# A fused attention and gated feed-forward kernel: a new order of the loads, the beginning and the first eight tiles

## The chip, the cores and the metric

The kernel runs on one core of a Trainium2 chip. The metric is the device time of one execution in microseconds (us). The core has five engines that work at the same time, each through its own list of instructions in order: TensorE (PE, products), VectorE (DVE), ScalarE (ACT), GpSimd (POOL) and SyncE (SP), which issues the loads and the transposes by DMA. Engines wait for each other by semaphores.

## The reference

```python
kv_pool = kv.reshape(B, H//4, 4, W//4, 4, C).mean(axis=(2, 4))
k = v = kv_pool.reshape(B, -1, C) @ w_sr            # 768 keys per batch
a = softmax(q @ k.T / sqrt(C));  x = a @ v          # 4 batches x 12288 rows, C = 128
x_prev = x shifted by one row (0 at a batch's start)
xk = mu_k*x + (1-mu_k)*x_prev;   xr = mu_r*x + (1-mu_r)*x_prev
out = sigmoid(xr @ w_r) * (relu(xk @ w_k)**2 @ w_v) # w_k 128x1024, w_v 1024x128
```

All of it is in float32; the kernel splits operands into a high and a low half and adds three products where one would lose digits.

## The kernel before

The 4 x 12288 rows are worked through in 96 tiles of 512 rows (the last one as two halves). Each tile is cut into small steps, each a named closure: `qf` loads the rows, `qh` and `ql` split them, `S0` to `S3` (with `SA0`, a first part) are the score products for four groups of 128 rows, `nm` is the row maximum on DVE, `ex` the exponential on ACT, `rc` the reciprocal sum, `f1` and `f2` split the softmax into two halves (tile `pp`), `tt` transposes `pp` by DMA into `pT`, `AV0` to `AV5` multiply it with the values (tile `px`), `xk` and `xr` mix neighbouring rows, `ha`, `hb`, `va`, `vb` and `z` are the feed-forward products, `o` and `so` the output.

No loop sets the order. Every step is put into one heap with a number, and `plan.give()` takes them out by that number; the engines' lists follow. The numbers stand in tables: `ONCE` for what is done once, `EARLY` for the first eight tiles (one dictionary each), `WHEN` plus 19.3 per tile for the tiles after, `LATE` for the last. The numbers are only a sequence, not times.

What is done once is of four kinds. Weights: `L_wk0`, `L_wk1`, `L_wv0`, `L_wv1` (512 KB each) and `L_wr0` (128 KB) are loaded as 64-bit words and put together on ACT and DVE (`wb`, `wl`, `wf`, `wu`, `ws`, `wt`, `we`, `wq`, `wp`); `wa` takes magnitudes (tile `wabs`) and `wc` sums their columns on PE into the PSUM tile `cs`; `wx` reads the largest sums from `cs` on DVE (tile `peak`). Keys of batch 0, the first 512 columns: `L_a0` to `L_a7` (512 KB each), each multiplied on PE as it lands (`pa0` to `pa7`, two products of two passes of 512 columns each), all into one sum. The other 256 columns: `L_b0` to `L_b2` (512 KB) and `L_b3`, `L_b4` (256 KB) are added up by DVE (`ab0` to `ab4`, tile `acc`) and multiplied afterwards (`pk1` for 192 columns, `pk2` for 64). From the key products ACT and DVE make `ks`, `ksh`, `kbl`; the exponent chain `ex` (five instructions on single columns, up to the reciprocal `ivs`) follows the maxima `am`. The key loads share six buffers: the seventh load waits until the first buffer has been read.

The fourth kind does no work of the reference: `id0`, `id1` and so on are products of the identity with itself, written into a part of `cs` that nobody reads.

```python
for j in range(IDLE):
    @once(f"id{j}")
    def _():
        for n in range(2):
            pe.matmul(column_sums(1), lhsT=ident, rhs=ident, start=True, stop=True)
...
dve.tensor_reduce(out=one("peak", n=3), in_=column_sums(), axis=AX.X, op=ALU.max)
```

`column_sums(1)` is the second half of `cs` and `column_sums()` a part of the first; both are one tile, so a product of `idN` that stands after `wx` waits until DVE has read. In float32 each such product is two passes of PE, so one `idN` is four.

Of the kernel before, what the change touches and what calls it, by code (L numbers as in the profile page):

```python
# [73 lines left out]
def tile_kernel(ctx, tc, qT, kv0a, kv0b, kvw, head, w_k, w_v, w_r, outT):  # L74
# [91 lines left out]
    def once(name):  # L166
        def put(fn):
            plan.add(ONCE[name], name, fn, ("once", 0))
        return put
# [31 lines left out]

    for j in range(IDLE):
        @once(f"id{j}")
# [871 lines left out]
    for i, (b, t0, T, at0) in enumerate(seq):  # L1075
# [26 lines left out]
IDLE = 24  # L1102
# [84 lines left out]
        "xek": 60.09518, "xk": 62.09518, "xkh": 68.09518, "xer": 72.09518, "xr": 82.09518,  # L1187
# [9 lines left out]
    },  # L1197
    {
# [7 lines left out]
        "AV5": 110.09518, "xcr": 114.09518, "xek": 129.09518, "xer": 130.09518, "xk": 137.09518,  # L1206
        "xr": 138.09518, "xkh": 149.09518, "xkl": 163.09518, "ha2": 188.49961, "xrh": 188.55182,
# [8 lines left out]
    },  # L1216
    {
# [270 lines left out]
```

## Time and profile before

| | |
|---|---|
| median of 3 runs | 1856.12 us (1855.11 to 1856.93) |
| span of the profiled execution, first to last instruction | 1854.3 us |
| PE busy | 1839.3 us, 9079 products |
| DVE, ACT, POOL busy | 1730.9, 1743.0, 1133.2 us |
| DMA | 252.52 MB, mean 136 GB/s |
| granted TensorE clock, mean | 1.000 |

The page gives the profiled execution's span, not its time by the runs' clock; a run's time also holds what lies around the span, and the median is 1.8 us above this span. Busy times are sums of one engine's instructions; where two engines are nearly full at once, a wait of one stage can still decide. Products are pipelined, so a row's duration is longer than the distance to the next one.

### The profile page before, as it was taken

The page shows a single profiled execution, that of the slowest core. Times are in us where ns is not written, and L with a number is a line of the kernel's source. Part 1 is how long each engine was busy: PE and PEld are TensorE (multiplying, and loading weights), DVE is VectorE, ACT ScalarE, POOL GpSimd, SP SyncE. Part 2 cuts the span into 40 slices and gives each one's busy share as a digit, 9 for nine tenths or more (in the row PEclk, how much of TensorE's full clock was granted, in tenths as well). Part 3 has the DMA queues.
Part 4 walks back from the last instruction along what each step waited for, and adds up shares of the span by engine and source line. Part 5 has one row for each costly group of instructions (what it writes and reads, how often), then busy time and mean ns, then how long its engine had stood idle before and what let it go on. Part 6 is the DMA issues. An engine that isn't in the chain of part 4 may idle for free.

```text
span 1854.3 us, 27743 instructions
## 1 busy us (share of the span) xinstructions
PE 1839.3 (99%) x9079; PEld 912.5 (49%) x9185; DVE 1730.9 (93%) x2811; ACT 1743.0 (94%) x2628; POOL 1133.2 (61%) x875
## 2 busy tenths in 40 slices
PE   9999999999999999999999999999999999999999
PEld 6444454444444444444444444444444444444445
DVE  8999999999999999999999999999998999899898
ACT  6999999999999999999999999999999999999997
POOL 1655565666666566666666666656666666666666
PEclk9999999999999999999999999999999999999999
DMA  7677575656667676656666676747565656555462
GB/s 248 142 154 160 130 166 125 129 128 131 135 138 168 142 159 148 134 118 128 137 127 164 142 170 141 161 103 142 123 136 120 128 128 125 120 109 114 91 126 57
DMA packets 654336, 252.52 MB, mean 136 GB/s; under 512 B 612080, under 2 KB 613104, under 8 KB 654192
## 3 DMA queue, kind: packets, MB, share of 16 engines
q1 hardware_dynamic: 654192, 250.75, 63.1%
q8 instruction: 72, 1.18, 0.3%
q14 instruction: 72, 0.59, 0.1%
HBM read 73.34 MB, written 25.17 MB: 53 GB/s over the span
## 4 chain that ended last, share of the span: by engine, by line
PE 89%; ACT 2%; issue 1%; DVE 0%; DVEq 0%; ACTq 0%
PE ph L39 25%; PE pv L39 24%; PE S L39 19%; PE px L39 18%; PE pz L39 3%; ACT rr L39 0%; ACT kh L39 0%; ACT pp L39 0%; PE pk L39 0%; ACT pe L39 0%; ACT kk L39 0%; ACT S L39 0%; ACT xer L39 0%; DVE pp L39 0%; DVE kk L39 0%
## 5 line engine op out<-in xcount | busy, mean ns | idle before, releaser
L39 POOL TENSOR_TENSOR kl<-kk,kh 128x1024 bf16<-128x1024 f32 (+1 forms) x291 | 617.9, 2124 | 129.4 <-ACT kh L39 112.6
L39 ACT ACTIVATE rr<-ph 128x1024 f32<-128x1024 f32 (+1 forms) x388 | 395.8, 1021 | 80.0 <-PE ph L39 76.8
L39 PE MATMUL px<-pT,vT 128*128 128x512 f16 (+1 forms) x1746 | 391.8, 377 | 2.1 <-DMA pT<-pp 2.1
L39 POOL TENSOR_TENSOR xrl<-xr,xrh 128x512 f16<-128x512 f32 (+1 forms) x97 | 144.9, 1494 | 275.1 <-DVE xrh L39 275.1
L39 ACT ACTIVATE kh<-rr 128x1024 f16<-128x1024 f32 (+1 forms) x291 | 306.5, 1055 | 0.7 <-PE pv L39 0.2
L39 PE MATMUL S<-kf,qh 128*128 128x256 f16 x1264 | 304.3, 326 | 0.0
L39 PE MATMUL ph<-xkh,wkl 128*128 128x512 f16 (+1 forms) x776 | 292.0, 377 | 0.4 <-DVE kk L39 0.2
L39 PE MATMUL pv<-kh,wvl 128*128 128x512 f16 (+1 forms) x776 | 291.9, 377 | 0.1
L39 PE MATMUL ph<-xkh,wkh 128*128 128x512 f16 (+1 forms) x776 | 291.9, 377 | 0.0
L39 PE MATMUL pv<-kh,wvh 128*128 128x512 f16 (+1 forms) x776 | 291.8, 377 | 0.0
L39 DVE SCALAR_TENSOR_TENSOR pp<-pe,rc,pp 128x768 f16<-128x768 f32 x289 | 286.9, 1011 | 0.5 <-ACT pp L39 0.5
L39 PEld LDWEIGHTS <-vT 128*128 128x128 f16 x1746 | 170.4, 98 | 205.9 <-issue 3.1
L39 ACT ACTIVATE pp<-pe,rc 128x768 f16<-128x768 f32 x289 | 263.8, 952 | 1.6 <-DVE rc L39 1.6
L39 DVE TENSOR_SCALAR_CACHE_REDUCE pe<-S,gs 128x768 f32<-128x768 f32 x238 | 238.0, 1015 | 25.5 <-PE S L39 25.4
L39 POOL TENSOR_TENSOR ql<-qf,qh 128x512 f16<-128x512 f32 (+2 forms) x97 | 141.9, 1463 | 195.1 <-ACT qh L39 195.1
L39 ACT ACTIVATE pe<-pe,nm 128x768 f32<-128x768 f32 x265 | 248.0, 936 | 0.3 <-DVE pe L39 0.3
L39 PEld LDWEIGHTS <-wkh 128*128 128x128 f16 x1552 | 151.8, 98 | 178.4 <-issue 0.7
L39 DVE TENSOR_TENSOR kk<-ph,rr 128x1024 f32<-128x1024 f32 (+1 forms) x194 | 233.9, 1206 | 3.9 <-ACT rr L39 3.2
L39 PE MATMUL ph<-xkl,wkh 128*128 128x512 f16 (+1 forms) x776 | 228.6, 377 | 0.0
L39 PE MATMUL S<-kf,ql 128*128 128x256 f16 x632 | 205.9, 326 | 4.1
L39 POOL TENSOR_TENSOR xkl<-xk,xkh 128x512 f16<-128x512 f32 (+1 forms) x97 | 145.1, 1496 | 103.0 <-DVE xkh L39 103.0
L39 PE MATMUL pv<-kl,wvb 128*128 128x512 bf16 (+1 forms) x681 | 193.0, 377 | 0.5
(152 smaller groups left out, 2937.5 us busy)
## 6 DMA issues: line engine op xcount, KB each, us to landing
qf<-qT SPq DMA_DIRECT2D x95, 256.0 KB, 3.6
outT<-o SPq DMA_DIRECT2D x95, 256.0 KB, 3.4
qm<-qT SPq DMA_DIRECT2D x78, 256.0 KB, 3.6
kvt<-kvw SPq DMA_DIRECT2D x36, 512.0 KB, 4.9
pT<-pp SPq DMA_TRANSPOSE x383, 4.0
kva<-kv0a SPq DMA_DIRECT2D x8, 512.0 KB, 9.4
kvb<-kv0b SPq DMA_DIRECT2D x3, 512.0 KB, 6.0
land<-moe_w_k SPq DMA_DIRECT2D x2, 512.0 KB, 6.2
```

The costliest lines, as they stand in the source:

```text
L39: return self.tc.keep_in_program_order(op(*args, **kwargs))
```

## The change

The instructions are the same; `IDLE` goes from 24 to 25, and the tables `ONCE` and `EARLY` get new numbers. `WHEN`, `LATE` and all code stay.

```diff
-IDLE = 24
+IDLE = 25
...
-    "id16": -145.90482, "id17": -144.90482, "id18": -143.90482, "id19": -142.90482,
...
-    "L_wk1": -137.90482, "L_b3": -136.90482, "mix": -135.90482, "L_wr0": -134.90482,
...
+    "L_wk1": -149.03887, "wb_wk1": -148.07774, "id0": -147.11661, "id1": -146.15548,
...
+    "id13": -41.39230, "pk1": -40.43117, "ks1": -39.47004, "am1": -38.50891, "ex": -37.54778,
+    "kb0": -36.58665, "wc_wv0": -35.62552, "wx": -34.66439, "id14": -33.70326, "id15": -32.74213,
```

The loads stood in the order wk1, b3, wr0, b4, a4, wv1, wk0, a6, a3, a7, wv0, a5, a0, a1, b2, a2, b1, b0; they now stand in the order wk1, wr0, wv1, b4, a6, b3, a3, wk0, a7, a5, a4, wv0, a2, a1, b2, b1, a0, b0. The eight key blocks are multiplied in the order a4, a6, a3, a7, a5, a0, a1, a2 before and a6, a3, a7, a4, a5, a2, a1, a0 now. The steps `idN` stood as 8 at the start, 3, 4 and 3 up to the first scores, then 3, 2 and 1 (24); they now stand as 9, 2, 1, 2 and 3, then 3, 2, 1 and 2 (25).

DVE's list near its beginning, before: the sums `ab3` and `ab4` (`acc<-kvb 128x32`) stand first, around a few instructions of the weights.

```order
L39 MEMSET mtop 128x1
L39 TENSOR_REDUCE acc<-kvb 128x32 [waits DMAHW2_49]
L39 TENSOR_SCALAR sign<-land 128x512 [waits DMAHW1_49]
L39 TENSOR_SCALAR mag<-mag 128x128 [waits Activation_49]
L39 TENSOR_SCALAR mag<-mag 128x128 [waits DVE_49]
L39 TENSOR_SCALAR mag<-mag 128x512 [waits Activation_49]
L39 TENSOR_SCALAR mag<-mag 128x512 [waits DVE_49]
L39 TENSOR_REDUCE acc<-kvb 128x32 [waits DMAHW4_49]
```

The same place now, with the end of what stands in front of them; PE's product on these sums (`pk2`) and the load `L_a4`, into the buffer of `L_b4`, wait for the second.

```order
L39 MEMSET mtop 128x1
L39 TENSOR_SCALAR mag<-mag 128x512 [waits Activation_49]
L39 TENSOR_SCALAR ei<-top 128x512
L39 TENSOR_SCALAR mag<-mag 128x512 [waits DVE_49]
L39 SCALAR_TENSOR_TENSOR top<-mag,sign 128x512 [waits DVE_49]
L39 TENSOR_TENSOR lf<-lf,ei 128x128
L39 TENSOR_SCALAR ei<-top 128x512 [waits DVE_49]
L39 TENSOR_REDUCE acc<-kvb 128x32 [waits DMAHW6_49]
L39 TENSOR_REDUCE acc<-kvb 128x32 [waits DMAHW4_49]
```

So 25 instructions of the weights and of `mix`, eight of them on 512 columns with one input and two with two inputs, moved ahead of the two sums.

PE's list in front of the first score product, before: the identity products (`cs<-ident`, six are three steps) wait for nothing.

```order
L39 MATMUL cs<-ones,wabs 128x1
L39 MATMUL cs<-ident 128x128 x6
L39 LDWEIGHTS ql [waits Pool_49]
L39 MATMUL S<-kbl,ql 128x512 [waits Activation_49]
L39 MATMUL S<-ksh,qh 128x512
L39 LDWEIGHTS qh
L39 MATMUL S<-kbl,qh 128x512 [waits DVE_49]
```

And now; all four groups of column sums stand ahead of it.

```order
L39 MATMUL cs<-ones,wabs 128x1
L39 MATMUL cs<-ident 128x128 [waits DVE_49]
L39 MATMUL cs<-ident 128x128 x5
L39 LDWEIGHTS ql [waits Pool_49]
L39 MATMUL S<-kbl,ql 128x512 [waits Activation_49]
L39 MATMUL S<-ksh,qh 128x512
L39 LDWEIGHTS qh
L39 MATMUL S<-kbl,qh 128x512
```

The first identity product now waits for DVE, and the score products stand behind it.

What it waits for stands on DVE here: `peak<-cs`, before, behind the first three row maxima (`nm<-S`).

```order
L39 RECIPROCAL ivs<-exs 128x1 [waits DVE_49]
L39 SCALAR_TENSOR_TENSOR kbl<-pk,ksh 128x192 [waits Activation_49]
L39 TENSOR_REDUCE nm<-S 128x1 [waits PE_49] x3
L39 TENSOR_REDUCE peak<-cs 128x3
L39 TENSOR_SCALAR rc<-sm 128x2 [waits Activation_49]
```

And now, behind the reciprocal of the exponent chain.

```order
L39 SCALAR_TENSOR_TENSOR kbl<-pk,ksh 128x512 [waits Activation_49]
L39 TENSOR_REDUCE tip<-ks 128x1 [waits Activation_49] x2
L39 TENSOR_REDUCE ex<-tip 128x1 [waits DVE_49]
L39 TENSOR_SCALAR ex<-ex 128x1 [waits DVE_49]
L39 TENSOR_SCALAR exi<-ex 128x1 [waits DVE_49]
L39 TENSOR_SCALAR exs<-exi 128x1 [waits DVE_49]
L39 RECIPROCAL ivs<-exs 128x1 [waits DVE_49]
L39 TENSOR_REDUCE peak<-cs 128x3 [waits PE_49]
L39 SCALAR_TENSOR_TENSOR kbl<-pk,ksh 128x192 [waits Activation_49]
L39 TENSOR_REDUCE nm<-S 128x1 [waits PE_49] x3
```

The reading of the column sums moved ahead of the three row maxima, and with it the place for which PE waits.

## Rows read from the trace of the kernel before

**Rows 1.** The page, busy us of each engine, share of the span, instructions

```profile
PE 1839.3 (99%) x9079; PEld 912.5 (49%) x9185; DVE 1730.9 (93%) x2811; ACT 1743.0 (94%) x2628; POOL 1133.2 (61%) x875
```

**Rows 2.** Windows: us; busy PE, PEld, DVE, ACT, POOL; PE clock; DMA share, GB/s

```profile
6.00:24.00 18.00, 16.01 (x63) 8.76 (x63) 17.09 (x40) 7.62 (x16) 0.00 (x0) 1.00 1.01 403
...
30.00:60.00 30.00, 27.98 (x160) 17.61 (x163) 28.76 (x55) 29.58 (x51) 14.79 (x17) 1.00 0.76 143
```

**Rows 3.** Tile views, loads `L_wk1` and `a7`: ns on SP, issued at, us to landing

```profile
L39 SPq DMA_DIRECT2D land<-moe_w_k x1: 416/416/416, 1.2 to 1.2; - x1
...
DMA to landing us min/median/max: 4.2/4.2/4.2
...
L39 SPq DMA_DIRECT2D kva<-kv0a x1: 328/328/328, 6.1 to 6.1; - x1
...
DMA to landing us min/median/max: 9.9/9.9/9.9
```

**Rows 4.** PE timeline: start us, us, out<-in, passes, idle before and releaser

```profile
1.34 6.43 PE L39 MATMUL cs<-ident 128*128 128x128 f32 x32 [1.34 <-POOL xek L39]
9.00 0.43 PE L39 MATMUL pk<-acc,first 128*128 128x64 f32 x2 [1.23 <-DVE acc L39]
...
13.52 5.42 PE L39 MATMUL pk<-kva,first 128*128 128x512 f32 x12 [0.53 <-DMA kva<-kv0a]
...
26.13 1.95 PE L39 MATMUL cs<-ident 128*128 128x128 f32 x16
...
29.87 0.38 PE L39 MATMUL S<-kbl,ql 128*128 128x512 bf16 x1
...
45.94 4.05 PE L39 MATMUL px<-pT,vT 128*128 128x512 f16 x18 [0.77 <-DMA pT<-pp]
...
55.58 2.10 PE L39 MATMUL px<-pT,vT 128*128 128x512 f16 x9 [0.84 <-DMA pT<-pp]
...
108.28 4.06 PE L39 MATMUL px<-pT,vT 128*128 128x512 f16 x18 [0.47 <-DMA pT<-pp]
```

**Rows 5.** DVE timeline, last key sums to the peak

```profile
25.02 2.50 DVE L39 TENSOR_REDUCE acc<-kvb 128x64 f32<-128x1024 f32 x2 [0.71 <-DMA kvb<-kv0b]
...
28.80 0.35 DVE L39 TENSOR_REDUCE tip<-ks 128x1 f32<-128x192 f32 x1
29.19 0.16 DVE L39 TENSOR_REDUCE ex<-tip 128x1 f32<-128x3 f32 x1
...
29.95 0.16 DVE L39 RECIPROCAL ivs<-exs 128x1 f32<-128x1 f32 x1
...
31.21 2.99 DVE L39 TENSOR_REDUCE nm<-S 128x1 f32<-128x768 f32 x3 [0.84 <-PE S L39]
34.12 0.17 DVE L39 TENSOR_REDUCE peak<-cs 128x3 f32<-128x24 f32 x1
```

**Rows 6.** DVE groups from 6 to 24 us: busy us, mean ns

```profile
L39 DVE SCALAR_TENSOR_TENSOR top<-mag,sign 128x512 int32<-128x512 int32 x4 | 2.7, 687 | 0.1
...
L39 DVE TENSOR_SCALAR sign<-land 128x512 int32<-128x512 int32 x4 | 1.7, 422 | 0.3 <-DMA land<-moe_w_k 0.3
...
L39 DVE TENSOR_REDUCE acc<-kvb 128x32 f32<-128x512 f32 x2 | 1.4, 682 | 2.6 <-DMA kvb<-kv0b 2.6
...
L39 DVE TENSOR_SCALAR sign<-land 128x128 int32<-128x128 int32 x1 | 0.2, 220 | 0.0
```

**Rows 7.** ACT timeline, from the last key block's product

```profile
26.33 0.60 ACT L39 ACTIVATE ksh<-pk 128x512 fp32r<-128x512 f32 x1 [3.73 <-PE pk L39]
...
27.30 0.62 ACT L39 CAST qh<-qf 128x512 fp32r<-128x512 f32 x1
...
28.44 0.33 ACT L39 ACTIVATE ks<-pk 128x192 f32<-128x192 f32 x1
```

**Rows 8.** Windows at the end, columns as in rows 2

```profile
1850.00:1851.00 1.00, 0.76 (x7) 0.43 (x5) 0.88 (x3) 0.00 (x0) 0.00 (x0) 1.00 0.00 0
...
1853.00:1854.30 1.30, 0.00 (x0) 0.00 (x0) 0.00 (x0) 0.00 (x0) 0.00 (x0) 0.66 0.00 0
```

More of the change, by code (lines that the diff above doesn't have):

```diff
@@ L1178 @@
     {
[8 rows of a table removed]
-        "xek": 60.09518, "xk": 62.09518, "xkh": 68.09518, "xer": 72.09518, "xr": 82.09518,
[9 rows of a table removed]
-    },
-    {
[7 rows of a table removed]
-        "AV5": 110.09518, "xcr": 114.09518, "xek": 129.09518, "xer": 130.09518, "xk": 137.09518,
-        "xr": 138.09518, "xkh": 149.09518, "xkl": 163.09518, "ha2": 188.49961, "xrh": 188.55182,
[8 rows of a table removed]
-    },
-    {
[8 rows of a table removed]
-        "xk": 188.68235, "xkh": 188.76067, "xkl": 188.81288, "xrh": 189.15226, "xrl": 191.57565,
[8 rows of a table removed]
-    },
-    {
[17 rows of a table removed]
-    },
-    {
[17 rows of a table removed]
-    },
-    {
[7 rows of a table removed]
-        "AV1": 227.56807, "xcr": 227.9118, "xek": 228.59238, "xk": 229.23924, "xer": 230.29038,
[9 rows of a table removed]
-    },
-    {
[7 rows of a table removed]
-        "AV1": 255.83824, "xek": 257.21489, "xck": 258.13266, "xer": 259.5141, "xk": 261.20005,
[9 rows of a table removed]
-    },
-    {
[17 rows of a table removed]
[8 rows of a table added]
+        "xk": 67.21539, "xer": 69.13765, "xkh": 73.94330, "xcr": 77.78782, "xkl": 79.71008,
[9 rows of a table added]
+    },
+    {
[8 rows of a table added]
+        "xk": 140.26128, "xkh": 145.06693, "xkl": 163.32840, "xrh": 188.56150, "ha2": 188.86088,
[8 rows of a table added]
+    },
+    {
[8 rows of a table added]
+        "xk": 188.74446, "xkh": 188.79435, "xrh": 189.84158, "xkl": 190.87958, "ha1": 193.37078,
[8 rows of a table added]
+    },
+    {
[17 rows of a table added]
+    },
+    {
[7 rows of a table added]
+        "AV1": 209.92953, "xer": 210.09664, "xcr": 210.23032, "xek": 210.43085, "xr": 210.49769,
+        "xk": 210.66479, "xkh": 220.22077, "xkl": 225.79970, "xrh": 228.36059, "xrl": 228.86190,
[8 rows of a table added]
+    },
+    {
[8 rows of a table added]
+        "xr": 228.97331, "xkh": 229.47462, "xrh": 229.53032, "xkl": 229.58602, "xrl": 229.64173,
[8 rows of a table added]
+    },
+    {
[17 rows of a table added]
+    },
+    {
[7 rows of a table added]
+        "AV4": 278.81470, "xcr": 279.60364, "xer": 279.72559, "xek": 280.54814, "xk": 280.56943,
[9 rows of a table added]
     },
```

330 rows, old and new, of tables (EARLY, ONCE) are left out of this document.

## The prediction

> **What bounds the kernel now.** I read the page's busy times first: TensorE (PE) is busy 1839.3 of 1854.3 us [rows 1]. The reader is to see that nearly everything after the beginning is PE at work, so a change of order can only win or lose where PE waits, or where it does products on the identity that nobody needs. The windows say where that is. While the loads run, PE has gaps, and the DMA engines move 403 GB/s at a share of 1.01: that stretch is full. From 30 to 60 us PE still lacks 2.0 of 30 us, while DVE is busy 28.76 and ACT 29.58 [rows 2]; there PE waits for the softmax of the first tiles.
>
> Then the timeline of PE. Its time before the first score product (S) at 29.87 splits into 32 passes on the identity (each step `idN` is two products of two passes), waits for the sum of the first key columns and for loads, a run of key products from 13.52 to 26.13 with nothing but the next block's pass behind each, 16 more passes [rows 4], and the six products, 12 passes, that stand ahead of S in the instruction stream. After S it stops before px (attention times values) for 0.77, 0.84 and, much later, 0.47 us, each time for a transposed tile [rows 4]. So the useful work up to S is about 15 us of 29.87; everything the order may win is in the other 15 and in those 2.1 us. What the loads need cannot be won.
>
> **The change, part by part.** *Loads.* The same 8.4 MB in another sequence. A block of 512 KB takes 1.3 us at 403 GB/s. The seventh big load of before, issued at 6.1, landed 9.9 later, at 16.0 [rows 3]; the sizes up to it add to 4.29 thousand KB; in the new order those same bytes end with key block a5. The next one, a4, needs the buffer of b4 and therefore DVE's sum `ab4`. If that sum is done before 16.0 less the time a load takes to start, the queue stays full. I get 13.6 for it (next part), so the last keys land as before (DVE's last two sums run from 25.02 to 27.52 [rows 5]): cost 0. Were the sum late, each us would move everything.
>
> *The beginning on DVE and PE.* Before, the two small sums stood first on DVE, and PE had its product on them at 9.00. Now 25 instructions of weights and mixing factors stand in front of them. DVE can start when the first weight block is there (issued 1.2, landing 4.2 later: 5.4 [rows 3]) and ACT has taken its magnitude (0.7): about 6.15. In front and with the sums are eight one-input instructions of 512 columns (0.42), two of two inputs (0.69), two sums (0.68) and fifteen small ones (0.22 at most) [rows 6]: 3.4 + 1.4 + 1.4 + 3.3 = 9.5 at most. They overlap: the 40 instructions of 6 to 24 us occupy 17.09 us [rows 2], and their means add to 19.7, a factor of 0.87. That gives 8.3 at most and 6.8 with the small ones at half the price; I take 7.4, between them, because about half of the small ones depend on the one before and can't overlap it. `ab4` ends at 6.15 + 7.4 = 13.6.
>
> PE meanwhile: 36 passes end at 8.2 (32 ended at 7.77; four more at 0.12 [rows 4]). Block a6 is 2.3 thousand KB ahead of the load of 16.0, at 403 GB/s 5.9 us earlier: 10.1. It is multiplied until 12.0, eight passes on the identity (16 took 1.95 [rows 4], so 0.12 each) go to 13.0, and the product on the sums waits until 13.6. Then seven blocks remain, as many as before from 13.52, where three took 5.3 (5.42 with the overlap at the row's end, 1.75 each) [rows 4]: 12.2. With the sum's product (0.3), four passes `id11` (0.5) and three short groups of column sums (0.4) they end at 27.0; before, the next thing started at 26.13. Term: **+0.9 us** (0 if the sum isn't waited for, +2.0 if DVE takes 8.3 and the column sums wait for ACT too).
>
> *From the last key block to S.* Before, S came 3.74 us after it (26.13 to 29.87). Its twelve passes stood ahead of the reading of the column sums (`wx`, the peak), which DVE did at 34.12, after three row maxima [rows 5]. Now `wx` stands on DVE behind the reciprocal of the exponent chain, and `id14` to `id16` stand on PE behind `wx`. They write the same tile that DVE reads, so PE's first pass there waits for DVE, and S stands behind it. The chain from 27.0: ACT starts 0.2 later and does ksh, ks and qh before the second part of ks; two such starts are 0.97 apart (26.33 to 27.30), so three take 1.46, and that last part takes 0.33 [rows 7]: 27.2 + 1.46 + 0.33 = 29.0. DVE's last maximum 0.35 + 0.05, then 29.19 to 30.11 as before for ex to the reciprocal, 0.92 [rows 5]: 30.4. The peak 0.17: 30.6. Twelve passes at 0.12: 1.46. S at **32.05**, 2.2 later than 29.87. Without the passes S could start when its keys and ql are there, near 30.2 by the same rows: here the products on the identity would be longer than the pause. Of the +2.2, 0.9 is the term above and **+1.3** is this one (-0.5 if S isn't held by the peak, +1.8 if ACT's order costs half a us more).
>
> *From S on.* DVE's list from the first row maximum to the end of tile 0's last split is the same but for the peak (0.17), which is now ahead: PE's stop before px moves with it. The four column sums that PE did between two parts of S (0.11) are also ahead. Together **-0.2**. There are 32 passes on the identity behind S instead of 24: eight more, 1.0 us of PE. I count them at nothing, because they lie in the waits before px, which were 2.1 us; if that cover were gone they cost 1.0. Later tiles have their own new order of the same instructions; the unchanged tables take over after the eighth tile. PE had one stop of 0.47 there and I leave that.
>
> Sum: 0.9 + 1.3 - 0.2 = **+2.0 us**: span 1854.3 to 1856.3. The median of the runs is 1856.12, 1.8 above the span of the profiled execution; so I predict **1858.1 us**. A run can tell it from no change from about 0.2% on, 3.7 us here: my forecast is inside.
>
> **The rivals.** *The waits don't count.* If `ab4` is there when PE comes and DVE reads the peak while ACT still works for S, S starts between 29.7 and 30.2; and the added passes fill stops that would be there anyway. The result is -0.7 to +0.5, about 1856 us. For it: my times on ACT and DVE add durations, and a chain of 5 us can be 1 us out. Against it: the wait is in the instruction stream, and every term that I can price makes DVE the later one.
>
> *The clock falls in a pause* (the slower side). The new order leaves PE idle from 8.2 to 10.1 and, with 0.3 of short products, from 28.6 to 30.6. The longest such gap before S now is 1.2 us (7.77 to 9.00 [rows 4]). PE's first 32 passes took 6.43 us, against 3.9 at the later price [rows 4]: a start at the lower of the two clocks (1.2 of 2.4 GHz) costs 2.5 us once. If the gap at 8.2 brings it back, the seven blocks slow down, and the sum becomes +4.5: 1860.6 us. It decides only if the clock falls in a gap like these. For it: at the end of the trace PE stops at 1850.8, and the granted clock averages 0.66 over the last 1.3 us [rows 8], so an idle PE does lose it. Against it: in the gaps that this trace has, up to 1.2 us, it stayed, and a product after 9.00 is as fast as a later one. The Trainium skill, page "TensorE: Matmul & The Clock Gate", section "HAM oscillation — how this bites in real kernels", says that waits between groups of products make the engine fall back to the slow clock and that each fall has to be paid again. By that rule this order's longer pauses are the risk, and the time would be the one just given; the trace agrees that an idle engine loses the clock, and shows no fall in a pause.
>
> *More waits in tiles 1 to 8* (also slower). DVE and ACT were full from 30 to 60 us, so an instruction that stands earlier for one tile is late for another; tile 1's last split now stands behind the scale factors and two row maxima. Two more stops of the 0.8 us kind and the uncovered passes (1.0) make +4.6: 1860.7.
>
> *Faster.* S as early as before, all three stops filled: -2.3, 1853.8, still inside 0.2%. A gain of 3.7 would need S three us earlier, against the loads.
>
> **How the numbers follow.** My forecast (+0.6 to +3.7) 0.52; waits that don't count (-2.5 to +0.6) 0.21; clock 0.09; more waits 0.12; a gain over 3.7 for a reason I don't see 0.06. The first two are inside 0.2%: faster 0.06, same 0.73, slower 0.21. The range leaves out 1 in 10 on each side: below, the case of stops filled, 1854.0; above, past the two slower rivals, 1861.5. The likeliest case's own range is 1856.7 to 1859.8.
>
> **What would show it.** In the changed kernel's PE timeline: 36 passes from 1.34, the product on the sums near 13.6 with DVE as releaser, the last key block's end near 27, an idle of about 2 us before twelve passes released by the peak, S near 32. The last two big loads should land at the same 25 to 26.5. If S starts before 31, the terms are too big; if passes after 10 us take 0.2 us, it was the clock; if S is at 32 and the end is not 2 us later, the stops after S gave it back. An earlier landing of the last keys would make me wrong altogether.

## The result and the profile after

The changed kernel takes 1868.88 us (median of 5 runs, 1866.78 to 1870.36) against 1855.87 us before (now five runs, 1855.11 to 1856.93): slower by 13.0 us, a ratio of 1.0069 with a 95% interval of 1.0056 to 1.0081. The prediction was 1858.1, its range ended at 1861.5. The profiled execution has a span of 1865.8 us, 11.5 more than before, and a granted clock of 1.000; PE is busy 1841.0 us, 1.7 more than before [rows 1], so most of it is idle time of PE. Of the five runs two had a mean clock of 1.000 (1866.8 and 1867.6 us) and three one of 0.998 or 0.999 (1868.9 to 1870.4).

PE's timeline of the changed kernel (start, duration, in brackets the idle time before and what ended it) answers to [rows 4]:

```profile
1.34 6.66 PE L39 MATMUL cs<-ident 128*128 128x128 f32 x36 [1.34 <-POOL ident masks.py:199]
...
10.25 1.95 PE L39 MATMUL pk<-kva,first 128*128 128x512 f32 x4 [2.24 <-DMA kva<-kv0a]
...
13.57 0.43 PE L39 MATMUL pk<-acc,first 128*128 128x64 f32 x2 [0.47 <-DVE acc L39]
...
25.65 1.98 PE L39 MATMUL pk<-kva,first 128*128 128x512 f32 x4 [0.56 <-DMA kva<-kv0a]
...
31.83 1.60 PE L39 MATMUL cs<-ident 128*128 128x128 f32 x12 [2.72 <-DVE peak L39]
33.27 0.38 PE L39 MATMUL S<-kbl,ql 128*128 128x512 bf16 x1
...
60.56 2.75 PE L39 MATMUL px<-pT,vT 128*128 128x512 f16 x12 [0.95 <-DVE xr L39]
...
88.76 0.28 PE L39 MATMUL S<-kbl,ql 128*128 128x256 bf16 x1 [0.89 <-POOL ql L39]
...
109.96 0.38 PE L39 MATMUL pz<-xrh,wrl 128*128 128x512 f16 x1 [0.73 <-DVE xr L39]
...
170.25 0.27 PE L39 MATMUL S<-kbl,ql 128*128 128x256 bf16 x1 [1.08 <-DVE pe L39]
```

The beginning has the forecast shape: 36 passes, the product on the sums at 13.57, and twelve passes released by the peak. But S stands at 33.27, 3.4 us later than before. And PE keeps stopping: all its stops of 0.14 us or more up to 360 us sum to 15.0 us (5.8 before), and 6.3 of them lie behind 60 us, where before had 0.65 (stops "after 60 us" are counted up to 360 us here and below).

Two stretches of before (first the length, then PE, PE's weight loads, DVE, ACT and POOL busy with counts, the clock, the DMA share and GB/s):

```profile
14.00:18.00 4.00, 4.00 (x11) 1.79 (x10) 3.91 (x9) 1.75 (x6) 0.00 (x0) 1.00 1.03 413
60.00:180.00 120.00, 118.83 (x579) 60.10 (x587) 115.68 (x168) 113.14 (x166) 69.13 (x55) 1.00 0.68 148
```

The same of the changed kernel:

```profile
14.00:18.00 4.00, 4.00 (x19) 2.09 (x18) 3.77 (x10) 3.06 (x7) 0.00 (x0) 1.00 0.93 315
...
60.00:180.00 120.00, 113.44 (x539) 55.98 (x549) 114.48 (x161) 107.75 (x158) 67.08 (x50) 1.00 0.62 139
```

From 60 to 180 us PE lacks 6.6 of 120 us instead of 1.2, while DVE looks as full as before. From 14 to 18 us the loads move 315 GB/s instead of 413: the load queue stood, because the load of a4, which waits for DVE's sum, was issued at 13.5. So the span's 11.5 us are 3.4 up to S, 5.4 from 60 to 180 us, and 2.7 between S and 60 us and elsewhere.

DVE's fullness there is not all work. Its timeline shows instructions on two columns that last 2 us:

```profile
77.52 1.97 DVE L39 TENSOR_SCALAR rc<-sm 128x2 f32<-128x2 f32 x1
...
106.96 2.10 DVE L39 TENSOR_SCALAR rc<-sm 128x2 f32<-128x2 f32 x1
```

The groups of DVE from 30 to 180 us (busy, mean ns of one, idle before) say how much that is. Before:

```profile
L39 DVE TENSOR_SCALAR rc<-sm 128x2 f32<-128x2 f32 (+1 forms) x17 | 3.7, 215 | 0.2 <-ACT pe L39 0.2
```

After, with the same seventeen instructions:

```profile
L39 DVE TENSOR_SCALAR rc<-sm 128x2 f32<-128x2 f32 (+1 forms) x17 | 11.3, 665 | 0.1
```

7.6 us more for the same work: a wait that the profile books as busy time. The first reading was that DVE stands there for ACT's exponential. The experiments were to show whether it was that.

### The profile page after: what moved, and what is told of

Same layout as the page of the kernel before. It is cut to its first block, busy times and chain, and to the rows that moved or that the text cites. A ratio compares the mean times of both kernels' runs of the same rounds, so it can differ in the third digit from the quotient of the medians.

```text
span 1865.8 us, 27751 instructions
## 1 busy us (share of the span) xinstructions
PE 1841.0 (99%) x9082; PEld 913.3 (49%) x9189; DVE 1738.5 (93%) x2811; ACT 1744.2 (93%) x2628; POOL 1135.0 (61%) x875
```

## The experiments

All times are medians with the ratio to the kernel before, which ran beside them at 1855.3 to 1855.8 us. The changed kernel's ratio, 1.0069, was taken in another session; differences between kernels of some 2 us are at the edge of what these intervals tell apart.

**Beginning and tiles apart.** Two kernels with the steps of both tables put in one line and cut at the first score product (numbers spread anew, so only the head of the first diff is shown; the second kernel has `IDLE = 26`).

```diff
-IDLE = 24
+IDLE = 23
```

> The new order up to the third of the steps id14 to id16, then everything that is left in the order of before (23 identity steps in all). Theory (the stops of tiles 1 to 8 belong to the order of those tiles, above all to DVE's reciprocal steps rc that stand before their exponentials are done): only the later start of S is left of the 13 us, 33.27 against 29.87 in the traces, so 1858 to 1860 us, and PE's stops after 60 us sum to about 1 us as in the trace of before (0.65), not 6.3. Rival (the late beginning upsets the tiles behind it, whatever their order): stops of 5 us or more after 60 us, 1865 to 1868 us.

> The order of before up to the first score product, then the new order of what is left. Theory (the order of tiles 0 to 7 is what costs): S starts near 29.9, the stops after 60 us stay at 5 to 6 us, and with the stops and added passes between S and 60 us the time is 1862 to 1866 us. Rival (the late beginning upsets the tiles): 1856 to 1859 us.

The new beginning alone takes 1861.21 us (1.0029, 1.0018 to 1.0040), the new rest alone 1863.31 us (1.0040, 1.0028 to 1.0053). 5.4 and 7.5 add up to nearly the whole 13.0. The first is 1.2 us above its expectation. From 60 to 180 us, the new beginning alone:

```profile
60.00:180.00 120.00, 119.85 (x589) 59.97 (x588) 116.67 (x172) 114.03 (x167) 69.09 (x54) 1.00 0.66 144
```

And the new rest alone:

```profile
60.00:180.00 120.00, 114.08 (x553) 56.27 (x552) 114.50 (x158) 106.63 (x155) 67.63 (x49) 1.00 0.62 138
```

PE's loss there goes with the tile order and hardly depends on when the tiles begin; most of its stops recur with the same length, 3.8 us earlier.

**The peak.** The three steps get numbers under that of `wx`; PE's list is the same, but DVE now waits for PE.

```diff
-    "kb0": -36.58665, "wc_wv0": -35.62552, "wx": -34.66439, "id14": -33.70326, "id15": -32.74213,
-    "id16": -31.78100, "kb1": -29.85874,
+    "kb0": -36.58665, "wc_wv0": -35.62552, "wx": -34.66439, "id14": -35.38524, "id15": -35.14495,
+    "id16": -34.90467, "kb1": -29.85874,
```

> The changed kernel, with id14 to id16 put ahead of the reading of the column sums; PE's list is the same, only who waits for whom is turned round: PE no longer waits for DVE's peak, DVE waits for PE. Theory (the peak sets S, as the wait of 2.72 us in the trace says): S starts when the subtracted queries are there, near 31.5 instead of 33.27, and PE's stop of 2.72 is gone; the kernel gains 1.0 to 1.8 us (1867 to 1868), since the later stops are of another origin. Rival (DVE and ACT set the pace there, and PE only waits somewhere else): S at 31.5 and the time within 0.5 us of the changed kernel.

1866.91 us (1.0057, 1.0045 to 1.0070), 2.0 less than the changed kernel. In its PE timeline the stop of 2.72 is gone and one of 0.97 for `ql` is left. S is only 0.9 earlier, because in this execution PE's first four key passes took 3.63 us:

```profile
10.18 3.63 PE L39 MATMUL pk<-kva,first 128*128 128x512 f32 x4 [2.01 <-DMA kva<-kv0a]
...
32.39 0.39 PE L39 MATMUL S<-kbl,ql 128*128 128x512 bf16 x1 [0.97 <-POOL ql L39]
```

The windows of the same execution show why (the third number from the right is the clock):

```profile
6.00:10.00 4.00, 2.18 (x16) 1.98 (x15) 3.83 (x21) 1.42 (x3) 0.00 (x0) 1.00 1.00 383
10.00:14.00 4.00, 3.82 (x8) 1.87 (x9) 3.90 (x9) 0.00 (x0) 0.00 (x0) 0.57 1.00 405
```

Behind an idle of 2.0 us PE was at the lower of its two levels for most of four microseconds.

**`rc` later.** Five `rc` steps (and one `f13`) get later numbers, each still ahead of its first user.

```diff
-"nm2": 17.23663, "rc1": 21.08115
+"nm2": 17.23663, "rc1": 29.25075
...
-"ex0": 201.05198, "rc1": 203.75078
+"ex0": 201.05198, "rc1": 206.34578
```

> The changed kernel, with the five rc steps on which DVE stood longest (1.24, 1.12, 1.97, 2.10 and 1.59 us, where 0.16 is usual) moved behind one to four other DVE instructions, each still ahead of its first user (and one f13 with it); PE's, ACT's and SP's lists are unchanged. Theory (DVE stands at rc for ACT's exponential, and what is queued behind it, nm, xr, xk and the splits, is what PE then waits for): the PE stops at 48.1, 60.6, 85 to 89, 110 to 111 and 160 us, 5.0 us in all, shrink to under 2; the kernel gains 3 to 5 us (1864 to 1866). Rival (DVE and ACT are full there, and a wait taken away at rc comes back at the next instruction): within 1 us of the changed kernel, 1868 to 1870.

1870.73 us (1.0083, 1.0070 to 1.0095), not faster. Three of the five fell to their usual length and tile 7's to 0.58, but what waits for `rc` on ACT and behind it was now late: PE stops 1.43 us ahead of px, 1.96 and 1.69 ahead of ph. And tile 5's `rc`, 6 us later and 4 us after ACT's last exponential before it (which ended at 109.01), still took 2.10 us, so the first reading falls. DVE of this kernel:

```profile
113.03 2.10 DVE L39 TENSOR_SCALAR rc<-sm 128x2 f32<-128x2 f32 x1
115.17 0.17 DVE L39 RECIPROCAL rc<-rc 128x2 f32<-128x2 f32 x1
```

POOL beside it:

```profile
112.71 2.40 POOL L39 TENSOR_TENSOR kl<-kk,kh 128x1024 bf16<-128x1024 f32 x1 [0.43 <-ACT kh L39]
```

It ends 0.02 us after POOL's instruction (115.13 and 115.11). In the changed kernel it is the same: 77.52 plus 1.97 is 79.49, 106.96 plus 2.10 is 109.06, and POOL has

```profile
77.33 2.12 POOL L39 TENSOR_TENSOR kl<-kk,kh 128x1024 bf16<-128x1024 f32 x1
...
106.80 2.25 POOL L39 TENSOR_TENSOR kl<-kk,kh 128x1024 bf16<-128x1024 f32 x1 [0.71 <-ACT kh L39]
```

which end at 79.45 and 109.05. Seven `rc` of the changed kernel up to 180 us lasted 0.4 us or more, and each of them began while a POOL instruction with two inputs (for `kl`, `ql`, `xkl` or `xrl`) ran and ended 0.02 to 0.03 us after it. Two runs test that: one moves `rc`, one leaves the order alone.

**`rc` earlier, ahead of POOL's instruction.** For tile 3 the exponential `ex0` moves ahead with it; tile 7 stays as in the run before.

```diff
-"nm2": 17.23663, "rc1": 21.08115
+"nm2": 17.23663, "rc1": 18.67833
...
-"ex0": 201.05198, "rc1": 203.75078
+"ex0": 201.05198, "rc1": 202.60898
```

> The changed kernel with the rc steps of tiles 1, 2, 3 and 5 moved one or two DVE instructions ahead, to a place at which GpSimd's long instruction has not begun in the trace (tile 7's stays as in the run with rc later). Theory after that run (rc is not held by an exponential: each of the long ones ends 0.02 us after a GpSimd instruction that was running when it began, so DVE and GpSimd are in each other's way): the four take 0.2 us instead of 1.2, 1.1, 2.0 and 2.1, DVE gets back 5.8 us, and the PE stops behind them shrink; 1865 to 1867 us. Rival (rc waits for ACT's sums, and an earlier place only waits longer): the four stay at 1 us or more, 1868 to 1871 us.

1864.70 us (1.0050, 1.0037 to 1.0063), 4.2 less than the changed kernel. Tile 1's, 2's and 5's `rc` are at their usual length, tile 3's at 0.78; the stops at 48, 60 and 110 us are gone.

**`rc` in another form, order untouched.** It leaves out the added 1e-9 in eight tiles.

```diff
-dve.tensor_scalar(rc, sm, 1e-9, 2.0 ** -15, op0=ALU.add, op1=ALU.mult)
+if i < len(EARLY):
+    dve.tensor_scalar(rc, sm, 2.0 ** -15, None, op0=ALU.mult, op1=ALU.add, accum_out=one(f"rs{i}_{s}"))
```

> The changed kernel with its order untouched, but the first half of rc in the first eight tiles written as the form with a running sum (times 2^-15, the added 1e-9 left out, one more number written): in the trace of before 254 instructions of that form ran while GpSimd was at work, and none took longer than usual. Theory (DVE's plain form can't run beside a GpSimd instruction): all eight long rc steps fall to 0.3 us or less at the same place, DVE gets back about 8 us, the PE stops after 60 us fall from 6.3 to under 3, 1863 to 1866 us. Rival 1 (rc waits for ACT): the long ones stay long, 1868 to 1870. Rival 2 (they get short and DVE and ACT set the pace elsewhere): stops after 60 us still 5 us or more, 1867 to 1869.

1863.40 us (1.0045, 1.0032 to 1.0059), 5.5 less. DVE from 30 to 180 us:

```profile
L39 DVE TENSOR_SCALAR_CACHE_REDUCE rc<-sm 128x2 f32<-128x2 f32 x16 | 2.4, 149 | 0.1
...
L39 DVE DVE_READ_ACCUMULATOR rc<-sm 128x1 f32 x16 | 1.3, 82 | 0.0
```

Not one of the sixteen is long (the longest 0.16), in the same place and order, and PE's stops after 60 us fall from 6.3 to 1.9. One of the long `rc` stands in the ninth tile, outside the edit, which the expectation overlooked; it kept the plain form and still took 1.05. Tile 3's, for one, stands at

```profile
77.39 0.14 DVE L39 TENSOR_SCALAR_CACHE_REDUCE rc<-sm 128x2 f32<-128x2 f32 x1
```

inside POOL's

```profile
77.37 2.14 POOL L39 TENSOR_TENSOR kl<-kk,kh 128x1024 bf16<-128x1024 f32 x1
```

where the plain form took 1.97.

> The order of before up to the first score product, the new order of the rest (1863.3 us by itself), and rc's first half in the other form. Theory (beginning and tile order add up, and of the tile order's 7.5 us the waits of rc beside GpSimd are the larger part): 1857 to 1859.5 us, PE stops after 60 us under 2.5. Rival (the gain of 5.5 us that the form had behind the new beginning needs that late beginning): 1861 to 1863 us.

With the old beginning the form brings the new tile order from 1863.31 to 1859.72 us (1.0019, 1.0010 to 1.0028), 0.2 above the expectation, and its stops after 60 us are 3.5, not under 2.5. Its five executions at a clock of 1.000 lie at 1857.8 to 1858.2, six at 0.999 at 1859.7 to 1860.5. The largest stop left is one for a transposed tile, which the new rest alone had too (1.83):

```profile
69.36 2.10 PE L39 MATMUL px<-pT,vT 128*128 128x512 f16 x9 [1.83 <-DMA pT<-pp]
```

> The kernel before, with rc's first half in the other form in the first eight tiles. In its trace rc was long only three times (0.48, 0.32 and 0.54 us), so theory: DVE gains 0.9 and pays 0.08 us sixteen times for the read of the sum; 1855 to 1856.5 us, no change. Rival (the other form is faster in itself, and that is why it gained 5.5 us in the changed kernel): 1851 to 1853 us.

1855.90 us (1.0001, 0.9992 to 1.0009): no change, so the form isn't faster by itself.

**The passes behind S.** All eight `idN` behind the first score product taken out (`IDLE` 17).

> The changed kernel without the eight identity steps behind the first score product (32 passes, 3.9 us of PE). Theory (they lie in time that PE would wait for the softmax anyway, as the prediction took it): 1868 to 1870 us, and the stops between 40 and 61 us grow by about 3 to 4 us. Rival (they delay score products on which DVE and ACT wait, so that most of their time is paid): 1865 to 1867 us. A second rival (without them the clock falls between 35 and 60 us): a granted clock under 1.00 there and over 1871 us.

1868.94 us (1.0071, 1.0059 to 1.0084), as the changed kernel, and its one execution at a clock of 1.000 takes 1866.99, where the changed kernel's two took 1866.78 and 1867.64: the passes cost nothing. PE's stops between 40 and 61 us grew by 2.4 us, less than expected. In the profiled execution the clock is 0.53 from 33 to 36 us, behind the wait for the peak; that isn't the second rival, because the run with `rc` in the other form has these passes and shows 0.50 at the same place.

**The pauses.** First the one at 8 us alone.

```diff
-IDLE = 25
+IDLE = 29
...
-"id8": -139.42757, "wf_wk1": -138.46644
+"id8": -139.42757, "id25": -139.23534, "id26": -139.04312, "id27": -138.85089, "id28": -138.65867, "wf_wk1": -138.46644
```

> The changed kernel with four more identity steps (16 passes, 1.95 us) right behind the first nine, where PE waits 2.24 us for key block a6 from 8.0 on. Theory (in some executions the clock falls in that pause: two profiled executions of edited kernels show 0.57 and 0.58 granted from 10 to 14 us, four key passes at 3.5 to 3.6 us instead of 1.95, and of the changed kernel's five runs two have a mean clock of 1.000 at 1867 us and three of 0.999 or 0.998 at 1869 to 1870 us): the clock stays at 1.00 from 10 to 14 us, no run is above 1868, and the median is 1866 to 1867 us. Rival (the difference between the runs comes from the loads): the spread stays 3 us or more and the median within 1 us of 1868.9.

1869.24 us (1.0076, 1.0064 to 1.0089), 1867.3 to 1871.5: a miss. The profiled execution keeps its clock at 10 us and loses it behind the other pause:

```profile
10.00:14.00 4.00, 3.14 (x15) 2.02 (x15) 3.93 (x11) 0.00 (x0) 0.00 (x0) 1.00 0.99 402
33.00:36.00 3.00, 3.00 (x14) 2.87 (x14) 0.24 (x1) 1.60 (x2) 3.00 (x3) 0.50 0.60 173
```

Then both pauses, with `rc` in the other form (the three diffs together):

> The changed kernel with all three: rc in the other form, id14 to id16 ahead of the reading of the column sums, and four more identity steps in PE's pause at 8 us. Theory (the clock falls in some executions in the pause at 8 us and in others in the one of 2.7 us before the score products, and both pauses are now filled): mean clock 1.000 in all runs, a spread under 1.5 us, and 1863.4 less the 2.0 us that the run with the passes ahead of the peak gained: 1860.5 to 1862 us. Rival (the clock falls for reasons of the chip, not of the pauses): runs at 0.998 or 0.999 remain, with a spread of 2 us or more.

1860.23 us (1.0025, 1.0015 to 1.0035), a little under the expected range. All nine executions have a mean clock of 1.000; their spread is 2.1 us, not under 1.5, so the clock wasn't all of it. With the old tile order behind it instead (and `rc` as it was):

> The new beginning in front of the old tile order, as in the first run (1861.2 us, mean clock below 1.000 in seven of eight executions), with id14 to id16 ahead of the reading of the column sums and four more identity steps in the pause at 8 us. Theory (the beginning's 5.4 us are the clock with 1 to 2, the peak's wait with 1 to 1.5, and the later keys with the rest): 1.000 in all runs, 1857.5 to 1859 us. Rival (the pauses moved nothing that PE would not have waited for elsewhere, ACT and DVE being late): 1859.5 to 1861 us at a clock of 1.000.

1858.29 us (1.0015, 1.0006 to 1.0024), ten of eleven executions at 1.000. So of the beginning's 5.4 us, 2.4 to 2.5 were the wait for the peak and the clock, and 2.9 remain.

**The loads.** The two sums earlier:

```diff
-"L_b3": -113.47706, "ab3": -112.51593, "ab4": -111.55480
+"L_b3": -123.80921, "ab3": -123.32864, "ab4": -123.56893
```

> The changed kernel with the two small key sums 14 DVE instructions earlier; nothing else moves (the issue of one load comes earlier in the list, not in the queue). Theory (the queue of loads stands until the sum frees the buffer for key block a4, issued at 13.5 us, and DMA moves 315 GB/s from 14 to 18 us where 413 were moved before): a4 is issued near 10.5 us, that stretch is back over 390 GB/s, the last loads land 0.7 to 1.2 us sooner, and with them S and the end: 1867 to 1868 us. Rival (the loads are not what the beginning waits for): the same stretch, S and time as in the changed kernel, 1868.5 to 1869.5 us.

1870.55 us (1.0077, 1.0063 to 1.0091): no gain. Loads are back at 409 GB/s from 14 to 18 us, as expected, but the weights stand behind the sums on DVE now, PE waits for their magnitudes with key blocks behind it, and the queue, which waits for these blocks' buffers, stands later:

```profile
14.00:18.00 4.00, 3.02 (x11) 1.39 (x9) 3.69 (x8) 1.25 (x4) 0.00 (x0) 1.00 1.02 409
22.00:26.00 4.00, 4.00 (x9) 1.75 (x8) 3.83 (x8) 0.63 (x1) 0.00 (x0) 0.84 0.05 20
```

PE's stop in this kernel:

```profile
19.59 0.28 PE L39 MATMUL cs<-ones,wabs 128*128 128x1 bf16 x5 [2.57 <-ACT wabs L39]
```

And the load of a0 alone, in the kernel with all three edits:

```diff
-"L_a0": -53.88699, "pa0": -52.92586
+"L_a0": -61.09547, "pa0": -52.92586
```

> The kernel with all three edits (1860.2 us, 1.000 in all runs), with the load of key block a0 ahead of those of b2 and b1; PE's, DVE's, ACT's and GpSimd's lists are the same. Theory (PE's stop of 0.56 to 0.91 us ahead of its last key block is only the late a0): that stop is gone, the last block ends 0.6 to 0.9 us sooner, S starts 0.5 to 0.9 us sooner, 1859.3 to 1859.8 us. Rival (DVE's last sums, now with later loads, become what S waits for): S within 0.3 us of 32.28 and 1860 to 1860.6 us. Second rival (the buffers make the queue wait): last loads later, over 1860.6 us.

1860.45 us (1.0025, 1.0015 to 1.0035), the first rival. PE no longer waits for a0, but for the sum of the last b block instead, and S is where it was:

```profile
29.27 0.59 PE L39 MATMUL pk<-acc,first 128*128 128x192 f32 x2 [0.97 <-DVE acc L39]
...
32.35 0.39 PE L39 MATMUL S<-kbl,ql 128*128 128x512 bf16 x1 [0.97 <-POOL ql L39]
```

## Why the prediction was wrong

**The step that failed** is "Later tiles have their own new order of the same instructions ... PE had one stop of 0.47 there and I leave that". That order costs 7.5 of the 13.0 us. The rival "more waits in tiles 1 to 8" named it, but as two stops and the uncovered passes, 2.6 us; the passes cost nothing and the stops after 60 us grew by 5.7. What makes most of them wasn't in the prediction at all: `rc`, an instruction of 0.16 us, did not run beside a GpSimd instruction, and where the new order lets it meet one, DVE stands for up to 1.9 us, with row maxima, `xr` and splits queued behind it. This is shown by the form: same order, no long `rc`, 5.5 us less. The rule was to be had. The Trainium skill, page "SBUF — State Buffer", section "Who interferes with whom", says that a plain `tensor_scalar` on DVE may need the port that it shares with GpSimd, that who comes first keeps it for the whole instruction, and that the form which also writes its accumulator does not; the traces here agree, with 2.10 us for the one and 0.15 for the other. The row was in the old trace too: three long `rc`, 0.9 us over their usual length in all.

What remains of the tile order, 2.6 us in executions at a clock of 1.000 (the run with the old beginning and the other form), is spread over stops such as those for `pT` (1.83) and `pe` (0.64 and 0.53), and wasn't traced further.

**"The beginning on DVE and PE", +0.9**: the sum's product came at 13.57, as worked out (13.6). The last block ended at 27.47 instead of 27.0, because PE waited 0.56 for a0.

**"Loads: cost 0"** was wrong too. I asked only that DVE's sum be done before 16.0 "less the time a load takes to start", and never priced that time. The sum was ready as worked out and a4 was issued at 13.54, but it landed at 17.43, 1.56 us after a5 (15.87), where blocks of this size land 1.3 apart while the queue is full: of its 3.9 us some 2.6 were the start (an estimate, 3.9 less the 1.3 of its bytes), and 2.3 were there. So the queue stood, and the rate from 14 to 18 us fell to 315 GB/s. It stood again for a0, which was issued at 21.61, after 3.7 us of waiting for PE, and landed 1.66 us behind the load before it. The last block landed at 27.07 instead of 26.27, outside the 25 to 26.5 that I had named as a sign, and DVE's last sum ended at 28.31 instead of 27.52 [rows 5].

**"From the last key block to S", +1.3**: the mechanism was right, PE waited for the peak, but from 27.47 to S it took 5.8 us instead of 5.0. In the chain I let ACT do ksh, ks and qh without a gap; it stood 0.76 for DVE's kbl, and the maxima came at 29.65:

```profile
29.02 0.60 ACT L39 ACTIVATE ks<-pk 128x512 f32<-128x512 f32 x1 [0.76 <-DVE kbl L39]
```

That kbl stands on DVE behind the last sum of keys, and so behind the last load:

```profile
27.09 1.22 DVE L39 TENSOR_REDUCE acc<-kvb 128x64 f32<-128x1024 f32 x1 [0.72 <-DMA kvb<-kv0b]
28.30 0.69 DVE L39 SCALAR_TENSOR_TENSOR kbl<-pk,ksh 128x512 bf16<-128x512 f32 x1
```

Before, ACT did ks at 26.82, ahead of DVE's kbl at 28.05:

```profile
26.82 0.59 ACT L39 ACTIVATE ks<-pk 128x512 f32<-128x512 f32 x1
```

```profile
28.05 0.68 DVE L39 SCALAR_TENSOR_TENSOR kbl<-pk,ksh 128x512 bf16<-128x512 f32 x1
```

In all traces with the new beginning kbl starts when the later of DVE's last sum and ACT's ksh of the last block is done, and ks follows it. So a0 alone moved nothing, because the sum then ended later, and S stays late with the peak and the clock taken out: in the run with both pauses filled and the old tiles, ks starts at 29.39 and S at 31.90, 2.0 later than in the trace of before. This is read from the traces, and no run moved kbl. How much of the 2.9 us that the beginning keeps it is stays open, because S varies by 1.1 us between the traces with the old beginning (28.75 to 29.87).

**"I count them at nothing"**, the passes behind S, held: 1868.94 without them.

**The clock** was a rival with 0.09. By the mean clocks it fell in three of the changed kernel's five runs, which are 2.3 us longer in the mean (1869.5 against 1867.2). Over all kernels with the new beginning and its two pauses, or with one of them left, 37 of 48 executions have a mean clock under 1.000; with the pause at 8 us shortened and the wait for the peak gone, 1 of 29; of 65 executions of before beside them, 4. "In the gaps that this trace has, up to 1.2 us, it stayed" was a true reading of one execution and no bound for gaps of 1.9 to 2.7 us. I named both pauses but priced a fall only at 8 us; the wait for the peak was a second place for it. The slow first passes that I took for the lower clock show it by their distance alone (0.21 us, later 0.11): the profile's clock reads 1.00 there, too.

No version here beats the kernel before; the best with the new beginning and the old tiles is 3 us behind.

## What to carry to other kernels

A new order of the same instructions must be priced over every stretch that it touches, not only where the diff is easy to read; a stretch that runs without stops is one in which the order can only lose. When a small instruction's mean grows in the list of groups, look at what the neighbouring engine runs at its end: a wait can be booked as busy time, and no list of waits names it. A pause of 2 us on PE costs more than its length in some executions, so judge it by the clocks of many runs, not by one profile.

## What was not expected of the hardware

The same 0.16 us instruction takes up to 2.10 us beside a GpSimd instruction and ends with it, while DVE's row maxima (0.95 us) and its `xk`, with one operand in PSUM (0.75 us), run beside one at their usual length. The clock's fall in a pause of 1.9 to 2.7 us is a matter of the execution: the changed kernel's profile shows 2.24 and 2.72 us at 1.00 throughout, other executions with pauses of 1.92 and 2.01 us at 8 us 0.58 and 0.57 from 10 to 14 us. In the run with the old beginning and the other form, six of eleven executions lost some clock at a place that its profile (1.00) doesn't show; that is open. It has a stop of 1.83 us at 69 us, which the kernels of the 1 of 29 don't have, but no trace shows the clock falling there.
